# Seven products of ones on TensorE ahead of the first column sum of a two-layer linear-attention and SwiGLU kernel

## Chip, cores and metric

The kernel runs on one core of one Trainium2 chip. The metric is the device time of one execution in microseconds (us), the median over several runs; lower is better. A profile is one further execution, recorded by the hardware profiler; its span goes from the first to the last instruction.

## What is computed

The input x has 2048 rows of 512 numbers in fp32. Two layers are applied, each an attention block and an MLP block with the same weights:

```python
x = x + attention(layernorm(x), wqkv, wo)
x = x + mlp(layernorm(x), w1, w3, w2)
x = x + attention(layernorm(x), wqkv, wo)
x = x + mlp(layernorm(x), w1, w3, w2)

# attention, 32 heads of 16; phi(t) = where(t > 0, t + 1, exp(t)) + 1e-6
kv  = einsum("bhsd,bhse->bhde", phi(k), v)
z   = einsum("bhsd->bhd", phi(k))          # column sums over all rows
num = einsum("bhqd,bhde->bhqe", phi(q), kv)
den = einsum("bhqd,bhd->bhq", phi(q), z) + 1e-6
attention = (num / den) @ wo
# mlp, 512 -> 1792 -> 512
mlp = (silu(x @ w1) * (x @ w3)) @ w2
```

## The kernel before, in words

Every matmul operand is split into a high and a low half in fp16, and each product is made of three passes (high x high, low x high, high x low); the helper `mm` at L518 issues these passes, so most matmuls of the trace carry that line.

Rows are worked on in 16 tiles of 128. In the attention of layer 0 a loop over the tiles t = 0 to 15 (the key loop in `attention`) does the following on TensorE for each tile: the key product into a fresh bank `pk` (12 matmuls of 128x512), then, for the tile before it, the column sums `z` as two matmuls of a matrix of ones against the high and the low half of phi(k) (`gram_sum`, L901, into the bank `pz`, which stays the same for the whole loop), then 12 matmuls that add phi(k) x normalised row into four banks `gt` (`gram`). For t = 0 there is only the key product, so the first sum stands behind the key products of t = 0 and t = 1. The first column sum has `start=True`: it overwrites the bank, the later ones add to it.

Between the key product and the sum, ScalarE and VectorE compute phi: three ACTIVATEs (L868, L869, L870), a combination on VectorE (L879), the cast to the scaled high half on ScalarE (L946, the first sum needs it) and the low half on VectorE (L961, the second sum needs it). In the same loop, other tiles are prepared: bn_stats and bn_aggr on VectorE (L480, L481), four small steps on GpSimd for the scale of the layer norm (L488 to L492), the normalise on ScalarE (L495), the split into halves and a transposing DMA.

The order of the work in both attention stages is written by hand: everything inside `in_order()` keeps, on each engine, the order in which the program issues it, also across what it traces before. The MLP stages are not inside it; there a planner (the tile framework with its timeline model) orders the instructions by priority and by the time at which the model thinks their inputs are ready.

Ahead of the key loop the program issues products of a matrix of ones (`keep_busy`, L1657, into a bank `warm` that nobody reads): 22 at the start and 10 after the first weight scale's product `pm_k`. The bank pool for `pk`, `pz`, `warm` and `pm_k` (`bank`) has four banks; `gt` comes from another pool of four.

Of the kernel before, what the change touches and what calls it, by code (L numbers as in the profile page):

```python
# [17 lines left out]
P = 128  # L18
# [70 lines left out]
def kernel(  # L89
# [10 lines left out]
    nc = tc.nc  # L100
# [26 lines left out]
    def acc_bank(name):  # L127
        return psum.tile([P, 512], F32, tag="acc", name=name)

    def bank(name):  # L130
        return psum.tile([P, 512], F32, tag="w", name=name)
# [170 lines left out]
    ones16 = const.tile([P, P], F16, name="ones16")  # L302
# [114 lines left out]
    def engine_of(what, i):  # L417
        table = {what: table_of(what, state["layer"])}
        return {"V": nc.vector, "P": nc.gpsimd, "A": nc.scalar}[table[what][i]]
# [52 lines left out]
    def ln_stats(t0, n):  # L472

        ln_moments(t0, n)
        ln_scale(t0, n)
# [37 lines left out]
    def mm(dst, lhs, rhs, n, first=True, last=True, shared=False):  # L513


        for k in range(n):
            for i, (a, b) in enumerate(PASSES):
                nc.tensor.matmul(  # L518
                    dst,
                    lhs(a, k),  # L520
                    rhs(b, k),
                    start=first and k == 0 and i == 0,
                    stop=last and k == n - 1 and i == len(PASSES) - 1,
                    skip_group_check=shared,
                )
# [197 lines left out]
    def fill(prep):  # L723

        at = state["fills"]
        state["fills"] += 1
        if prep is None and "rows" not in state:
            return
        for tasks in prep or ():
            tasks.calls += 1  # L730
        table = FILLS[0 if prep is not None else 1]
        for which in table[at].strip("-") if at < len(table) else "":
            if which == "r":
                if "rows" in state:
                    next(state["rows"], None)
            elif prep is not None:
                if which == "1":
                    settle()
                prep[int(which) - 1].step()

    def next_tick(prep):
        if prep is not None:
            for tasks in prep:
                tasks.tick += 1
# [117 lines left out]
    def phi_act(ps, u, eps, in_bank=False):  # L862

        e, r = f32("kept"), ps if in_bank else f32()
        if eps:
            nc.scalar.activation(e, ps, AF.Relu, scale=info["nuk"])  # L868
            nc.scalar.activation(r, ps, AF.Identity, scale=u, bias=one_eps)  # L869
            nc.scalar.activation(e, e, AF.Exp, scale=-1.0)  # L870
        else:
            nc.scalar.activation(e, ps, AF.Exp, scale=u)
            nc.scalar.activation(r, ps, AF.Relu, scale=u)
        return e, r

    def phi_sum(e, r, eps, to=None):
        to = e if to is None else to
        if eps:
            nc.vector.scalar_tensor_tensor(to, e, EPS, r, OP.add, OP.max)  # L879
        else:  # L880
            nc.vector.scalar_tensor_tensor(to, e, 1.0, r, OP.min, OP.add)
        return to

    def attention(layer, ready, prep, before_gram):
# [5 lines left out]
        gt, pz, pks = [], [], {}  # L890
# [6 lines left out]
        def gram_sum(t):  # L897
            if sums[t] == "E":
                pk = pks[t]
                for a in range(2):  # L900
                    nc.tensor.matmul(  # L901
                        pz[0],
                        ones16,
                        pk[:, a, :],
                        start=t == sums.index("E") and a == 0,
                        stop=not rows_of and t == NT - 1 and a == 1,
                    )

        def gram(t):
            pk, nat = pks.pop(t), nats.pop(t)  # L910
            for j in range(NK):
                mm(
                    gt[j],
                    lambda a, k: nat[:, a, j * P : (j + 1) * P],
                    lambda b, k: pk[:, b, :],
                    1,
                    first=t == 0,
                    last=t == NT - 1,
                )

        for t in range(NT):
            if t:
                next_tick(prep)
            if layer == 0 and t == 12:
                nc.sync.dma_start(att_d["k"], wk_s)
            xt = xts.pop(t)
            pp = bank("pk")
            mm(pp, lambda a, k: xt[:, a * NK + k, :], lambda b, k: wk_s[:, b, k, :], NK)
            before_gram(t)
            if t == lag:  # L930
                gt.extend([acc_bank(f"gt{j}") for j in range(NK)])
                if "E" in sums:
                    pz.append(bank("pz"))
                for i in range(lag):
                    gram(i)
            if lag < t < LATER:
                gram_sum(t - 1)
                gram(t - 1)
            elif t > LATER:
                gram_sum(t - 2)  # L940
                gram(t - 2)
            e, r = phi_act(pp, info["uk"], True)
            pk = pks[t] = pk_ring.next(F16, 2, D)

            def high():
                nc.scalar.activation(pk[:, 0, :], e, AF.Copy, scale=info["tk"])  # L946
                if sums[t] != "E":
                    engine = engine_of("pz", t)
                    if t == rows_of[0]:
                        engine.tensor_copy(pksum, e)  # L950
                    else:
                        engine.tensor_tensor(pksum, pksum, e, OP.add)

            def turn():
                if t + 3 < NT:
                    keys_turn(t + 3, xts, nats)
                elif t + 3 - NT < 3:
                    load_query(t + 3 - NT)

            def low():  # L960
                nc.vector.scalar_tensor_tensor(  # L961
                    pk[:, 1, :], e, info["tk"], pk[:, 0, :], OP.mult, OP.subtract
                )

            steps_ = {
                "r": lambda: t + 3 < NT and keys_rows(t + 3),
                "s": lambda: phi_sum(e, r, True),
                "h": high,
                "t": turn,
                "l": low,  # L970
                "n": lambda: t + 4 < NT and ln_stats(t + 4, 1),
                "f": lambda: fill(prep),
            }
            for name in (KEYS[layer] if layer or t > 1 else FIRST[t]).split():
                steps_[name]()
# [147 lines left out]
    def keys_rows(t, xn=None):  # L1123

        xn = f32() if xn is None else xn
        xns[t] = xn
        normalise(xn, t)
# [3 lines left out]
    def keys_turn(t, xts, nats):  # L1131

        xn = xns.pop(t)
        xts[t] = xk_ring.next(F16, 2 * NK, P)
        nats[t] = nat = ring["nat"].next(F16, 2, D)
        high_part("key", t, nat[:, 0, :], xn)
        engine_of("keylow", t).tensor_tensor(nat[:, 1, :], xn, nat[:, 0, :], OP.subtract)
        last["t"] = nc.sync.dma_start_transpose(xts[t], nat.rearrange("p a d -> p (a d)"))
        keep_transposed(t, xts[t])
        issue_loads(t)  # L1140
# [27 lines left out]
    def load_query(t):  # L1168
        xqs[t] = xq_ring.next(F16, 2 * NK, P)
        nc.sync.dma_start(xqs[t], xt_d[:, t])  # L1170
# [288 lines left out]
    def pair(layer, ready, prep, before_gram):  # L1459
        state["layer"] = layer  # L1460
        if layer == 0 or PIN1:
            with in_order():
                attention(layer, ready, prep, before_gram)
        else:
            attention(layer, ready, prep, before_gram)
        return mlp(layer, prep)
# [175 lines left out]
    for item in LOADS[0].split():  # L1642
        what, t = item.split(":")
# [100 lines left out]
```

## Time and profile before

| | us |
|---|---|
| median of 3 runs | 1183.33 |
| lowest and highest run | 1180.77, 1184.78 |
| the profiled execution, its own time | 1182.41 |
| the profiled execution, span | 1180.7 |
| TensorE matmuls busy | 1148.0 (97%) |
| VectorE, ScalarE, GpSimd busy | 831.0, 638.8, 420.6 |
| mean granted TensorE clock | 0.999 |

In the rows below PE is TensorE's matmuls, PEld its weight loads, DVE VectorE, ACT ScalarE, POOL GpSimd, SP SyncE. A row of the view in order of time merges neighbouring instructions of one kind: start, duration of the whole merged piece, engine, line, operation, output<-inputs, shape, count, and in brackets the idle time of the engine before it and what ended that. A matmul's duration includes its way through the array, so consecutive ones overlap: their step from start to start is shorter than the duration of one.

### The profile page before, as it was taken

To read this page: it belongs to the slowest core of one execution; us is meant where nothing else is said; L and a number is where in the kernel's file an instruction comes from. 1 tells how busy PE (TensorE), PEld (TensorE's weight loads), DVE (VectorE), ACT (ScalarE), POOL (GpSimd) and SP (SyncE) were. 2 spreads that over 40 slices of the span, in tenths; PEclk is the share of its full clock that TensorE was granted. 3 is DMA by queue.
4 is the path that set the end of the run, shared out by engine and by line. 5 is a ranking of instruction groups with operands and counts; after the bars stand their busy time and mean duration, and the time that the engine had idled before them with its cause. 6 is when DMAs were issued, how large, how long until landed. Compare 5 with 4: busy or idle time off the path is not lost.

```text
span 1180.7 us, 21818 instructions
## 1 busy us (share of the span) xinstructions
PE 1148.0 (97%) x8868; PEld 863.3 (73%) x8868; DVE 831.0 (70%) x1383; ACT 638.8 (54%) x1078; POOL 420.6 (36%) x488
## 2 busy tenths in 40 slices
PE   8999998899999999999999999999999999999998
PEld 3444444788888888888864454467888888888887
DVE  6778898977877886767774559756855775756543
ACT  5777687856544454434456644775544344443422
POOL 5342589402000144235268714684542210102010
PEclk9999999999999999999999999999999999999999
DMA  8977575979542221111416434664351350121000
GB/s 258 342 207 245 113 171 110 270 246 294 159 143 99 81 81 64 63 64 64 81 53 180 103 110 105 130 156 112 99 139 64 126 188 26 57 79 37 1 37 37
DMA packets 163396, 147.43 MB, mean 125 GB/s; under 512 B 129632, under 2 KB 138976, under 8 KB 158688
## 3 DMA queue, kind: packets, MB, share of 16 engines
q1 hardware_dynamic: 163296, 146.04, 42.7%
q8 instruction: 69, 1.13, 0.4%
q14 instruction: 31, 0.25, 0.1%
HBM read 72.48 MB, written 42.07 MB: 97 GB/s over the span
## 4 chain that ended last, share of the span: by engine, by line
PE 60%; DVE 15%; ACT 7%; POOL 6%; DMA 6%; issue 3%; SPq 1%; POOLq 0%; ACTq 0%; DVEq 0%
PE bb L518 16%; PE po L1381 13%; PE bc L518 8%; PE gt L518 5%; PE pk L518 5%; PE ba L518 4%; PE po L518 3%; PE pq L518 3%; DMA arena<-arena 3%; DMA arena<-in_B_w_dram 3%; PE po L1401 2%; DVE arena L1290 2%; DVE arena L1337 2%; DVE arena L442 2%; DVE arena L1430 2%
## 5 line engine op out<-in xcount | busy, mean ns | idle before, releaser
L518 PEld LDWEIGHTS <-arena 128*128 128x128 f16 x6360 | 618.3, 98 | 257.0 <-issue 16.1
L518 PE MATMUL bb<-arena 128*128 128x256 f16 x2688 | 329.5, 273 | 6.6 <-ACT arena L1334 4.0
L1381 PE MATMUL po<-arena 128*128 128x256 f16 x1932 | 234.6, 273 | 9.0 <-ACT arena L1293 6.4
L1381 PEld LDWEIGHTS <-arena 128*128 128x128 f16 x1932 | 187.8, 98 | 35.5 <-ACT arena L1293 9.3
L1295 DVE TENSOR_TENSOR arena<-arena 128x512 f16<-128x512 f32 (+1 forms) x104 | 114.5, 1100 | 105.5 <-ACT arena L1293 105.2
L1334 ACT ACTIVATE arena<-bb 128x512 f32<-128x512 f32 x196 | 114.8, 589 | 122.8 <-PE bb L518 82.1
L518 PE MATMUL bc<-arena 128*128 128x256 f16 x1344 | 165.8, 273 | 0.7 <-ACT arena L1334 0.5
L1293 ACT ACTIVATE arena<-arena 128x512 f16<-128x512 f32 x112 | 99.8, 891 | 120.4 <-DVE arena L1308 46.9
L1289 ACT ACTIVATE arena<-arena,scalars 128x512 f32<-128x512 f32 x112 | 74.7, 667 | 116.0 <-DVE arena L1337 115.5
L1290 DVE SCALAR_TENSOR_TENSOR arena<-arena,scalars 128x512 f32<-128x512 f32 x112 | 88.5, 790 | 51.7 <-ACT arena L1289 51.6
L1337 DVE TENSOR_TENSOR arena<-arena,bc 128x512 f32<-128x512 f32 x112 | 76.5, 683 | 55.0 <-ACT arena L1334 44.4
L1450 POOL TENSOR_TENSOR arena<-arena 128x512 f32<-128x512 f32 x25 | 35.2, 1409 | 207.6 <-DVE arena L1430 207.6
L1430 DVE SCALAR_TENSOR_TENSOR arena<-po,scalars,arena 128x256 f32<-128x256 f32 (+1 forms) x170 | 92.1, 585 | 9.1 <-PE po L1381 7.6
L518 PE MATMUL pk<-arena 128*128 128x512 f16 x384 | 89.8, 384 | 2.2 <-DMA arena<-arena 2.1
L518 PE MATMUL po<-arena 128*128 128x512 f16 x384 | 87.8, 379 | 3.2 <-DMA arena<-arena 2.1
L518 PE MATMUL gt<-arena 128*128 128x512 f16 x384 | 87.8, 379 | 0.6 <-ACT arena L946 0.4
L518 PE MATMUL pq<-arena 128*128 128x512 f16 x384 | 87.6, 379 | 0.1
L518 PE MATMUL ba<-arena 128*128 128x256 f16 x672 | 87.1, 273 | 0.0
L1305 POOL TENSOR_TENSOR arena<-arena 128x256 f32<-128x256 f32 x15 | 11.9, 792 | 148.7 <-DVE arena L1290 148.7
L495 ACT ACTIVATE arena<-arena,nb_all,rs_all 128x512 f32<-128x512 f32 x64 | 50.5, 807 | 26.5 <-POOL nb_all L492 26.3
L1401 PE MATMUL po<-arena 128*128 128x256 f16 x480 | 56.8, 273 | 0.4 <-ACT arena L1293 0.4
L1276 POOL TENSOR_TENSOR arena<-arena 128x512 f16<-128x512 f32 (+2 forms) x33 | 47.4, 1460 | 26.0 <-DMA arena<-arena 19.8
(163 smaller groups left out, 1289.4 us busy)
## 6 DMA issues: line engine op xcount, KB each, us to landing
arena<-xb_d SPq DMA_DIRECT2D x12, 1792.0 KB, 7.1
xb_d<-arena SPq DMA_DIRECT2D x8, 1792.0 KB, 5.9
xt_d<-arena SPq DMA_DIRECT2D x32, 256.0 KB, 2.9
arena<-xt_d SPq DMA_DIRECT2D x32, 256.0 KB, 3.3
arena<-in_B_w_dram SPq DMA_DIRECT2D x8, 896.0 KB, 6.7
arena<-in_B_w_dram SPq DMA_DIRECT2D x28, 256.0 KB, 3.4
w_d<-arena SPq DMA_DIRECT2D x4, 1792.0 KB, 10.8
arena<-w_d SPq DMA_DIRECT2D x4, 1792.0 KB, 6.7
```

The costliest lines, as they stand in the source:

```text
L495: nc.scalar.activation(dst, x_sb[:, t, :], AF.Identity, scale=rs_all[:, t : t + 1], bias=nb_all[:, t : t + 1],)
L518: nc.tensor.matmul(dst, lhs(a, k), rhs(b, k), start=first and k == 0 and i == 0, stop=last and k == n - 1 and i == len(PASSES) - 1, skip_g ...
L1276: engine_of("rowlow", 2 * c + j).tensor_tensor(nat[:, 1, lo:hi, :], s, nat[:, 0, lo:hi, :], OP.subtract)
L1289: nc.scalar.activation(t, gate, AF.Silu, scale=info["u1"])
L1290: nc.vector.scalar_tensor_tensor(t, up, info["hid"], t, OP.mult, OP.mult)
L1293: nc.scalar.activation(hs[:, 0, lo:hi], t[:, lo:hi], AF.Copy)
L1295: engine.tensor_tensor(hs[:, 1, lo:hi], t[:, lo:hi], hs[:, 0, lo:hi], OP.subtract)
L1334: nc.scalar.activation(dst, bank_, AF.Copy)
L1337: nc.vector.tensor_tensor(dst, dst, bank_, OP.add)
L1381: nc.tensor.matmul(po[:, i * HALF : (i + 1) * HALF], hs[:, a, qx, cs], w2[:, b, qw, :], start=g == ends[0] and i + a + b == 0, stop=g == e ...
L1401: nc.tensor.matmul(acc[n][:, half * HALF : (half + 1) * HALF], hs[:, a, qx, cs], w2_a21[g][:, b] if (i, half) == (0, 1) else w2[:, b, i + ...
L1430: nc.vector.scalar_tensor_tensor(dst, src, cb, to, OP.mult, OP.add)
```

## The change

At t = 1 of layer 0's key loop, behind the key products and ahead of the first column sum, seven products of ones with ones are issued into the bank `pz`. Each starts and stops its own accumulation, and the first column sum, which has `start=True`, overwrites what they leave.

```diff
                 for i in range(lag):
                     gram(i)
+            if layer == 0 and t == 1:
+
+                for _ in range(7):
+                    nc.tensor.matmul(
+                        pz[0].rearrange("p (a n) -> p a n", a=4),
+                        ones16,
+                        ones16[:, None, :].to_broadcast([P, 4, P]),
+                        start=True,
+                        stop=True,
+                    )
             if lag < t < LATER:
                 gram_sum(t - 1)
                 gram(t - 1)
```

## Rows read from the trace of the kernel before

**Rows 1.** The page: busy time by engine, and the clock in 40 slices.
```profile
PE 1148.0 (97%) x8868; PEld 863.3 (73%) x8868; DVE 831.0 (70%) x1383; ACT 638.8 (54%) x1078; POOL 420.6 (36%) x488
...
PEclk9999999999999999999999999999999999999999
```

**Rows 2.** TensorE's matmuls in order of time, 12 to 26 us.
```profile
12.17 5.35 PE L518 MATMUL pk<-arena 128*128 128x512 f16 x24
19.40 0.38 PE L901 MATMUL pz<-arena,ones 128*128 128x512 f16 x1 [1.88 <-ACT arena L946]
20.19 0.38 PE L901 MATMUL pz<-arena,ones 128*128 128x512 f16 x1 [0.41 <-DVE arena L961]
20.40 2.75 PE L518 MATMUL gt<-arena 128*128 128x512 f16 x12
22.99 2.75 PE L518 MATMUL pk<-arena 128*128 128x512 f16 x12
```

**Rows 3.** The chain that ended last, 15 to 26 us: start, us, what.
```profile
15.44 0.60 DVE st L480
...
17.70 0.20 POOL nb_all L492
...
17.93 0.81 ACT arena L495
18.74 0.62 ACT arena L946
...
19.39 0.76 DVE arena L961
...
20.19 0.38 PE pz L901
20.57 2.59 PE gt L518 x12
23.16 2.59 PE pk L518 x12
```

**Rows 4.** All engines in order of time: the products of ones at the start.
```profile
3.78 0.15 PEld L1657 LDWEIGHTS <-ones 128*128 128x128 f16 x1 [0.28 <-issue]
4.21 0.15 PEld L1657 LDWEIGHTS <-ones 128*128 128x128 f16 x1 [0.28 <-issue]
...
9.71 2.32 PE L1657 MATMUL warm<-ones 128*128 128x512 f16 x10
```

**Rows 5.** The line of the sums: operation, count, ns min/median/max, first and last start.
```profile
L901 PE MATMUL pz<-arena,ones x32: 376/379/379, 19.4 to 106.9; 128*128 128x512 f16 x32
```

**Rows 6.** Stretches around the wait: busy us of PE, PEld, DVE, ACT, POOL; PEclk; DMA share; GB/s.
```profile
12.00:17.50 5.50, 5.36 (x25) 2.37 (x25) 4.67 (x15) 4.62 (x8) 2.17 (x4) 1.00 0.83 228
17.50:20.20 2.70, 0.41 (x3) 0.10 (x2) 1.60 (x4) 2.27 (x4) 1.62 (x4) 1.00 1.07 286
20.20:26.00 5.80, 5.80 (x27) 2.63 (x27) 2.14 (x4) 2.56 (x5) 3.15 (x6) 1.00 1.01 328
```

**Rows 7.** ScalarE in order of time, 14 to 24 us.
```profile
15.55 0.77 ACT L869 ACTIVATE arena<-pk,scalars 128x512 f32<-128x512 f32 x1
...
18.65 0.70 ACT L946 ACTIVATE arena<-arena,scalars 128x512 f16<-128x512 f32 x1
19.26 0.67 ACT L868 ACTIVATE arena<-pk,scalars 128x512 f32<-128x512 f32 x1
```

**Rows 8.** TensorE in order of time at 44 us.
```profile
44.72 4.45 PE L518 MATMUL pk<-arena 128*128 128x512 f16 x12 [2.08 <-DMA arena<-arena]
```

**Rows 9.** Stretches of half a us there, columns as in rows 6.
```profile
44.50:45.00 0.50, 0.28 (x2) 0.17 (x3) 0.42 (x1) 0.50 (x2) 0.00 (x0) 1.00 1.03 393
45.00:45.50 0.50, 0.50 (x4) 0.24 (x3) 0.50 (x2) 0.44 (x2) 0.00 (x0) 0.85 1.06 406
45.50:46.00 0.50, 0.50 (x3) 0.20 (x2) 0.47 (x2) 0.50 (x2) 0.00 (x0) 0.50 1.03 397
...
48.50:49.00 0.50, 0.50 (x3) 0.14 (x2) 0.50 (x2) 0.00 (x0) 0.00 (x0) 0.73 1.33 352
49.00:49.50 0.50, 0.50 (x4) 0.25 (x3) 0.50 (x1) 0.29 (x1) 0.00 (x0) 1.00 1.02 386
```

**Rows 10.** TensorE in order of time at 199 us.
```profile
199.58 1.25 PE L518 MATMUL bb<-arena 128*128 128x256 f16 x10 [2.07 <-DMA arena<-arena]
200.67 1.26 PE L518 MATMUL ba<-arena 128*128 128x256 f16 x10
```

**Rows 11.** The stretch behind it, columns as in rows 6.
```profile
199.50:204.00 4.50, 4.42 (x41) 3.96 (x41) 3.27 (x8) 3.32 (x7) 4.50 (x5) 1.00 0.52 117
```

**Rows 12.** TensorE's waits from 200 us to the end: us in total, times, longest.
```profile
PE po L1381 <- ACT arena L1293: 6.4, 9, 1.8
PE bb L518 <- ACT arena L1334: 4.0, 5, 1.6
```

## Prediction

> **What bounds the kernel now.** I read the page first: its table of busy time, the clock row of its 40 slices, then the waits of TensorE, and only then the microseconds around the edit. The page says that TensorE's matmuls are busy for 97% of the span and that no other engine passes 70% [rows 1]. So a change in the number or the place of matmuls counts where TensorE is late, and is free where it sits idle. The edit stands in the key loop of layer 0 at t = 1, between the 24 products of the first two key tiles and the first column sum. TensorE's rows in order of time show the place: the `pk` products run from 12.17 us and end at 17.52, then the engine is idle for 1.88 us until the first sum starts at 19.40, idle again for 0.41 us, and the second sum starts at 20.19 with the twelve `gt` products right behind it [rows 2]. The chain that ended last tells what the two waits are: it does not run through TensorE before 20.19. It runs through bn_stats of tile 3, GpSimd's four small steps, ScalarE's normalise at L495, its key cast at L946 (0.62 us on the chain) and VectorE's low part at L961 (0.76 us), and only then through the second sum [rows 3]. L495 and L946 sit in ScalarE's queue in that order, so the first sum waits for a normalise of another tile, not for more matmul time. TensorE's idleness here is a symptom; filling it shortens none of these steps.
>
> **The change, part by part.** It removes nothing and moves nothing. It adds seven matmuls of 128x512 with their seven weight loads, on TensorE alone: no DMA, nothing on VectorE, ScalarE, GpSimd or SP.
>
> Their price: the same form stands in the kernel as `warm`. Ten of them, at the clock's upper level, took 2.32 us in all [rows 4], and one alone lasts 379 ns by the row of the sums [rows 5], so the step from start to start is (2.32 - 0.38) / 9 = 0.216 us. Seven cost 7 x 0.216 = 1.51 us of issue. The first can start one step after the last `pk` product started, 17.52 - 0.38 + 0.216 = 17.36 us; the seventh starts at 17.36 + 6 x 0.216 = 18.65 and ends at 19.03. The first sum is released at 19.40, 0.37 us after that. **Cost on the path: 0.** What hides them is the 1.88 us wait, and if that cover shrank there is a second one: the second sum is held by L961 until 20.19, so the first sum could start as late as 20.19 - 0.216 = 19.97 for nothing. Seen from the step at which the queue is free (18.87), the cover left is 19.97 - 18.87 = 1.10 us, five more products.
>
> The bound above: the products at the lower level of 1.2 GHz. At the start of the kernel weight loads of the same stream are 0.42 to 0.43 us apart [rows 4]. Seven at 0.43: the seventh starts at 17.36 + 6 x 0.43 = 19.94, the first sum at 20.37, the second at 20.80, against 20.19: 0.61 us late. I take the upper level, since the granted clock is 1.00 in the stretch before, in it and after it [rows 6], and the 24 products before it ran at it, (5.35 - 0.38) / 23 = 0.216 us apart [rows 2]; 0.61 us stays for the range.
>
> Waits added: the seven write a bank that was handed out at t = 0 and that nobody reads before the end of the loop; their operand `ones16` was set at the start. The two tiles made in `bank` before the key tiles, `warm` and `pm_k`, end by 9.71 + 2.32 = 12.03 us [rows 4], and the first two `pk` tiles are alive beside it. The sum that follows is on the same engine and starts its bank anew. So the wait for L946 stays where it is, on the first sum, and the seven stand before it in the queue. Bound of an unseen wait: the bank could at worst be free when ScalarE's reads of the first key tile end (15.55 + 0.77 = 16.32) [rows 7], still before 17.36. Cost 0. Nor does anyone wait for the seven: ScalarE takes the second key tile only at 19.26, behind L946 [rows 7], although its products ended at 17.52.
>
> What they could give is the clock, and here the trace has three waits of about this size. After 2.08 us of idleness TensorE resumed at 44.72; the granted clock fell to 0.50 soon after and came back at about 48.8, and the twelve products took 4.45 us [rows 8, 9] instead of the 2.75 us of the same row elsewhere [rows 2]: 1.70 us lost. After 2.07 us, ended at 199.58, the clock stayed at 1.00 and the products ran at full speed [rows 10, 11]. After our 1.88 + 0.41 us it stayed at 1.00 too [rows 6], and the `gt` and `pk` rows behind it read 2.75 us [rows 2]. So equal idleness can end either way, and in this execution there is nothing at this place to win back. **Gain: 0 here; up to 1.70 us in an execution where the clock does fall here.** I take 0, the row of this very place, and keep 1.70 for the range.
>
> The Trainium skill, in "TensorE: Matmul & The Clock Gate", Part 1, under "What's actually happening", says that the window in which the chip judges activity runs free and does not restart with a kernel. That agrees with the two waits of 2.07 and 2.08 us that ended differently. By that rule the same wait may lose the clock in one execution and keep it in the next, and the sum would be 0 in some and -1.70 us in others; the profile shows one execution only.
>
> **Sum.** 1182.41 us (the profiled execution, span 1180.7 plus 1.7 around it) + 0 - 0 = 1182.4 us. That is 0.9 below the median of the three runs, 1183.33, and inside their spread of 1180.77 to 1184.78.
>
> **The rivals.**
>
> *A: the fall of the clock at this place is usual, and the change removes it.* For: the three runs spread over 4.0 us, more than two falls at 1.70; one of the three similar waits shows a fall, and ours is in two pieces, so the whole of it (17.52 to 20.19) is the longest thin stretch of the three: TensorE is busy for 0.41 of 2.70 us in it [rows 6]. Against: the only execution I can see keeps the clock. If the median run of before holds the fall, after is 1183.33 - 1.70 = 1181.6 us. Behind 20.19 the chain is TensorE's through the sums, `gt` and `pk` [rows 3], so the loss would be carried on.
>
> *B: slower, by the order of the MLP.* Only the attention stages are written in a fixed order; the MLP's instructions are ordered by a planner with a timeline model of its own. If the model believes that the seven products push TensorE back, the instructions of the MLP could come out in another order. The price is bounded by the largest waits of TensorE there, 6.4 us for L1293's cast ahead of the output products and 4.0 us for L1334's copies [rows 12]; an order that doubles both gives 1182.4 + 10.4 = 1192.8 us. It decides as soon as TensorE's idle time before L1381 and `bb` grows by 3.5 us. Against: the seven lie on one engine, in a wait, with a fixed order over the whole attention stage that follows, so all engines should enter the MLP as before.
>
> *C: the same with the other sign.* An order that halves both waits gives 1182.4 - 5.2 = 1177.2 us. It needs the same accident.
>
> *D: the change doesn't do what it says:* the seven run at the lower level, or wait for the bank, and hold the sums back. By the bound above this is +0.6 us, 1183.0, inside what can be told from nothing.
>
> **How the numbers follow.** Forecast (nothing moves), 1182.4 us: 0.58. A, 1181.6: 0.22. D, 1183.0: 0.05. B, 1192.8: 0.08. C, 1177.2: 0.07. A measurement of this kernel tells some 0.3%, 3.5 us, from no change. Only C and B lie beyond that, so faster 0.07, slower 0.08, same 0.85. The range: the lowest run shown less one fall avoided, 1180.77 - 1.70 = 1179.1, to the highest run shown with one more fall elsewhere, 1184.78 + 1.70 = 1186.5. It holds the forecast, A and D, 0.85 in all, and leaves B and C out.
>
> **What would show it.** In the trace of after: a row of seven matmuls into `pz` from `ones` between 17.3 and 19.1 us, the first sum at 19.40 and the second at 20.19 as before, the `gt` and `pk` rows behind them at 2.75 us, TensorE's busy time up by about 1.5 us and its wait for L946 down from 1.88 to about 0.4 us, with the span unmoved. The weight loads of the seven should be some 0.2 us apart. The fall of the clock after 44.72 may or may not be there. Wrong it would be if the sums start later than 20.19 (cost of the products), if the same fall is gone from later stretches with the time down by 1.70 us or a multiple (A, more widely than I think), or if the output products' waits in the MLP differ by more than a few tenths (B, C).

## The result and the profile after

Twenty runs of each kernel: before 1181.91 us in the median, after 1184.39 (1182.19 to 1187.36). The ratio is 1.0018, with a 95% interval of 1.0012 to 1.0025: the change costs some 2 us. That is less than the 3.5 us that the prediction called "no change", but it is clear of the noise of so many runs. The profiled execution of after took 1186.52 us (span 1184.7).

The lines that answer to [rows 2] and [rows 8], TensorE's matmuls of after in order of time (start us, us, what, count, and in brackets the idle time before and what ended it):

```profile
17.22 1.67 PE L939 MATMUL pz<-ones 128*128 128x512 f16 x7
19.26 0.38 PE L901 MATMUL pz<-arena,ones 128*128 128x512 f16 x1 [0.37 <-ACT arena L956]
20.05 0.38 PE L901 MATMUL pz<-arena,ones 128*128 128x512 f16 x1 [0.41 <-DVE arena L971]
20.26 2.75 PE L518 MATMUL gt<-arena 128*128 128x512 f16 x12
...
29.12 2.76 PE L518 MATMUL pk<-arena 128*128 128x512 f16 x12 [0.49 <-DMA arena<-arena]
...
47.41 4.45 PE L518 MATMUL pk<-arena 128*128 128x512 f16 x12 [3.76 <-DMA arena<-arena]
```

The first four rows are as forecast: the seven take 1.67 us, end 0.37 us ahead of the first sum, and the second sum still starts 0.79 us after the first. (The line numbers of after are 10 higher behind the edit.) What differs comes 9 and 27 us later. The `pk` products of t = 3, which waited for nothing in before, wait 0.49 us for their transposing DMA, and those of t = 6 wait 3.76 us instead of 2.08 and start at 47.41 us instead of 44.72: 2.69 us late. The program order of every engine is the same in both kernels but for the seven products and their weight loads, the waits as well. So this is no new order (rivals B and C are out); a transfer has become later.

Which one, the first reader of the first w1 block on VectorE tells. The block is 896 KB of the MLP's weights, which the key loop loads ahead; the reader is L360, a maximum over the block, and it stands in VectorE's queue ahead of the key tile's phi. First before, then after:

```profile
27.20 2.08 DVE L360 TENSOR_REDUCE pt_w<-arena 128x1 f32<-128x896 f32 x2 [0.47 <-DMA arena<-in_B_w_dram]
```
```profile
28.21 2.08 DVE L360 TENSOR_REDUCE pt_w<-arena 128x1 f32<-128x896 f32 x2 [1.64 <-DMA arena<-in_B_w_dram]
```

The block lands 1.0 us later, and VectorE, whose queue is in order, hands that on to L879, to the statistics and the keys of the next tiles, and through these to the issue of later DMAs. And SyncE (SPq is its queue), which issues all DMAs, is held longer by a transposing DMA of that time. First before, then after:

```profile
25.97 1.34 SPq L1138 DMA_TRANSPOSE arena<-arena  x1
28.24 0.33 SPq L1156 DMA_DIRECT2D xt_d<-arena  x1
```
```profile
25.82 2.42 SPq L1148 DMA_TRANSPOSE arena<-arena  x1
29.13 0.33 SPq L1166 DMA_DIRECT2D xt_d<-arena  x1
```

How that becomes 2.69 us at t = 6 stands in SyncE's rows and in the chain that ended last. SyncE issues a further block of weights (L533) and then the transposing DMA of t = 6 (L1138, L1148 in after). First before, then after; the last line of each is that DMA's way from issue to landing:

```profile
37.32 0.46 SPq L533 DMA_DIRECT2D arena<-in_B_w_dram  x1
38.86 1.23 SPq L1138 DMA_TRANSPOSE arena<-arena  x1
...
38.86 5.81 DMA arena<-arena
```
```profile
38.72 0.45 SPq L533 DMA_DIRECT2D arena<-in_B_w_dram  x1
39.28 2.15 SPq L1148 DMA_TRANSPOSE arena<-arena  x1
...
39.28 8.09 DMA arena<-arena
```

The transposing DMA is issued only 0.42 us later, but lands at 47.37 instead of 44.67 us, 2.70 us later. In all fourteen profiled executions of this document it lands 0.8 to 1.0 us behind the block issued ahead of it. That block is issued 1.40 us later, and it takes 7.68 instead of 6.54 us (by its landing in the trace's semaphore records). Why it takes 1.14 us longer, no run shows; the next fetch of TensorE's program lies at 58.5 us in both.

One thing in the DMA queues had moved. The page's DMA part counts a queue `q8 instruction`, with 69 packets of 16 KB; TensorE has 17736 matmuls and weight loads, 257 to a packet, so I take these packets for TensorE's own program. In the stretch from 24.5 to 27 us (queue and kind: packets, MB, share of 16 engines), before shows no such packet, and after shows one; from 28 to 30.5 us it is the other way round. First after at 24.5 to 27, then before at 28 to 30.5:

```profile
q1 hardware_dynamic: 562, 0.73, 150.6%
q8 instruction: 1, 0.02, 2.3%
```
```profile
q1 hardware_dynamic: 378, 0.99, 100.2%
q8 instruction: 1, 0.02, 2.4%
```

2.3% of 16 engines for 2.5 us is 0.92 us of one DMA engine. The seven products are 14 instructions (a weight load and a matmul each), and with 14 more ahead of it TensorE's stream asks for a 16 KB block earlier: at 24.92 us, amid the first w1 block and the transposing DMA of t = 3, instead of at 28.52, behind both (they landed at 27.17 and 28.18). The other instruction queue, q14, is no such sign: its packet near 40 us starts at 41.6 us in before and at 39.7 in e5_count, which are equally fast.

The clock: after shows a fall behind the wait near 47 us, like before, and none near 20 us. In this execution a second one follows at 235 us, behind a wait of 2.59 us for L1344. The kernel is 2.69 us behind where the first `kv` product starts (120.96 against 118.26 us), and 4.08 us behind at the last matmul (1180.67 against 1176.60); the 1.4 us between come with that second fall. Such a fall near 235 us also stands in e2_after and e7_fillB_after below, but not in e11_after nor in any of the other ten executions; so it may well have a part in the median, which the profiles can't tell.

### The profile page after: what moved, and what is told of

Same layout as the page of the kernel before. It is cut to its first block, busy times and chain, and to the rows that moved or that the text cites. A ratio compares the mean times of both kernels' runs of the same rounds, so it can differ in the third digit from the quotient of the medians.

```text
span 1184.7 us, 21832 instructions
## 1 busy us (share of the span) xinstructions
PE 1152.1 (97%) x8875; PEld 865.3 (73%) x8875; DVE 830.6 (70%) x1383; ACT 637.7 (54%) x1078; POOL 420.5 (35%) x488
## 4 chain that ended last, share of the span: by engine, by line
PE 62%; DVE 15%; DMA 7%; ACT 7%; POOL 4%; issue 3%; SPq 2%; POOLq 0%; ACTq 0%; DVEq 0%
PE bb L518 16%; PE po L1391 13%; PE bc L518 8%; PE pk L518 5%; PE gt L518 5%; PE po L518 5%; PE pq L518 4%; PE ba L518 4%; DMA arena<-arena 3%; DMA arena<-in_B_w_dram 3%; PE po L1411 2%; DVE arena L1300 2%; DVE arena L1347 1%; DVE arena L442 1%; DVE arena L1440 1%
## 5 line engine op out<-in xcount | busy, mean ns | idle before, releaser
L1344 ACT ACTIVATE arena<-bb 128x512 f32<-128x512 f32 x196 | 114.7, 588 | 122.9 <-PE bb L518 82.8
L1347 DVE TENSOR_TENSOR arena<-arena,bc 128x512 f32<-128x512 f32 x112 | 76.4, 682 | 55.5 <-ACT arena L1344 44.9
```

The lines of the kernel that those rows point to most:

```text
L1344: nc.scalar.activation(dst, bank_, AF.Copy)
L1347: nc.vector.tensor_tensor(dst, dst, bank_, OP.add)
```

## The experiments

Two theories were put to the test. **T, the traded fall:** the thin stretch near 20 us does make the clock fall in many executions of before, but the time lost comes out of the later wait, and the change only moves the fall there. **F, the moved fetch:** the 14 further instructions move a program fetch into the critical transfers. The rivals stand with each expectation. Every kernel does the whole computation; only products that nobody reads are added or taken away. F came up after the first four runs; theory I of these four (the instructions themselves do harm) is its forerunner.

**e1_before, e2_after.** The two kernels once more.

> The kernel before once more, with its clock in every run. Theory T (traded fall): the thin stretch between 17.5 and 20.2 us costs before a fall of the clock in a good part of its executions, that fall is absorbed by the later 2 us wait for the transposing DMA, and executions with it show no second fall at 45 us; so its runs show one fall (mean clock 0.999) or none, seldom two, median about 1181.9 us. Theory I (more instructions): the mean clock is no different from that of after.

> The changed kernel once more. Theory T: median about 1184.4 us, the clock lower than in before by one fall in many runs (0.997 to 0.998), a fall behind the wait near 45 us, none near 20 us. Theory I (the 14 further instructions themselves do harm): 1184.4 us too, whatever the clock does.

Measured: e1_before 0.9995 of before [0.9985, 1.0005], e2_after 1.0014 [1.0006, 1.0023]. Over these twelve runs of each kernel the mean clocks are the same, 0.998. Over all runs on record they are not: 0.9987 for before (108 runs) and 0.9981 for after (40 runs). One fall costs 1.70 us, 0.0014 of the span, so after has some 0.4 of a fall more in a run (an estimate from these numbers). What also differs is where the falls lie. This execution of the unchanged kernel has the fall near 20 us:

```profile
19.27 0.38 PE L901 MATMUL pz<-arena,ones 128*128 128x512 f16 x1 [1.88 <-ACT arena L946]
20.06 0.38 PE L901 MATMUL pz<-arena,ones 128*128 128x512 f16 x1 [0.41 <-DVE arena L961]
20.28 4.44 PE L518 MATMUL gt<-arena 128*128 128x512 f16 x12
...
44.53 2.76 PE L518 MATMUL pk<-arena 128*128 128x512 f16 x12 [0.39 <-DMA arena<-arena]
```

The `gt` products lose 1.69 us (4.44 against 2.75), and the wait near 45 us shrinks by the same 1.69 (0.39 against 2.08), so that TensorE resumes at 44.53, no later than the 44.72 of [rows 8], and no fall follows there. The span is 1178.8 us, 1.9 less than that of before's first profile, which had the fall behind the wait. In this execution the fall near 20 us is not only free, it goes with none near 45. (A later one, at 197.9 us, costs 1.71 us in its rows, and the two waits for L1334 and L1235 behind it shrink from 1.01 + 1.16 us in before to 0.59 in all.)

**e3_tiny7, e4_four.** The edit with seven products of 16 columns, and with four full products.

```diff
-                for _ in range(7):
+                for _ in range(4):          # e4_four
...
-                        pz[0].rearrange("p (a n) -> p a n", a=4),
+                        pz[0][:, :16],      # e3_tiny7
                         ones16,
-                        ones16[:, None, :].to_broadcast([P, 4, P]),
+                        ones16[:, :16],     # e3_tiny7
```

> The seven products with 16 columns instead of 512: the same instructions in number, order, bank and waits, but next to no time of the array, so the idle stretch stays. Theory T: like before, about 1182 us (within 0.7). Theory I (instructions, bank or queue do the harm): like after, about 1184.4 us.

> Four products instead of seven: the idle stretch before the first sum is 1.0 us instead of 0.4 us. Theory T: the fall behind it becomes rare already, so like after or in between, 1183 to 1184.4 us. Theory I: in between by number, 1183.3 us.

Measured: e3_tiny7 1.0003 [0.9991, 1.0016], e4_four 1.0012 [1.0001, 1.0023]. By its time e3_tiny7 is as T had it, 1182.84 us beside 1182.60 of before, although its interval reaches up to the lower half of after's; e4_four fits both. So the times speak for T, if anything. But the traces give what was missing: in e3_tiny7 the clock fell at 19.8 us, as in e1_before, and yet the wait near 45 us was 1.93 us and not 0.4. The fetch is at 25.67 us here and at 26.06 in e4_four. Something that comes with the instructions and not with their array time seemed to make transfers late.

**e5_count.** The seven products stay; 14 instructions go from the start, where 22 products of ones become 9 and three fp32 products (an fp32 product is two weight loads and two matmuls, and about four times as long: five take 4.45 us in e6_long_count).

```diff
-        keep_busy(22)
+        keep_busy(9)
+        for _ in range(3):
+            nc.tensor.matmul(
+                warm.rearrange("p (a n) -> p a n", a=4),
+                ones,
+                ones[:, None, :].to_broadcast([P, 4, P]),
+                start=True,
+                stop=True,
+            )
```

> The changed kernel, but of the 22 products of ones at the start 13 are replaced by three fp32 products of about the same total time, which takes 14 instructions out of TensorE's stream ahead of the seven: its 16 KB instruction fetches should be back where before has them. Theory F (moved fetch): in before that fetch lies near 28.5 us, in after near 24.9, amid the load of the first w1 block and a transposing DMA; with the count restored it lies at 28.5 again, the w1 block lands near 27.2, the wait ahead of the pk products at 45 us is about 2 us instead of 3.4 to 3.8, and the time is 1.5 us below after, about 1182.5 us. Rival (the fetch is a bystander, only the clock matters): 1184 us as after, wait of 3 us or more.

Measured: 1.0000 of before [0.9991, 1.0009], 1181.73 us beside 1181.34. The fetch is back behind 28 us (the q8 line is of the stretch 28 to 30.5), the block lands when it did, and the wait is 2.47 us:

```profile
q8 instruction: 1, 0.02, 2.7%
```
```profile
27.00 2.08 DVE L360 TENSOR_REDUCE pt_w<-arena 128x1 f32<-128x896 f32 x2 [0.61 <-DMA arena<-in_B_w_dram]
```
```profile
17.28 1.67 PE L939 MATMUL pz<-ones 128*128 128x512 f16 x7
19.07 0.38 PE L901 MATMUL pz<-arena,ones 128*128 128x512 f16 x1
...
44.93 4.45 PE L518 MATMUL pk<-arena 128*128 128x512 f16 x12 [2.47 <-DMA arena<-arena]
```

With the count of instructions restored, the seven products cost nothing and bring nothing: the forecast of the prediction, but for the fetch. F's rival, as it was put (1184 us and a wait of 3 us or more), falls. The clock did change, too: its mean is 0.9994 over these twelve runs, against 0.9987 of before on the same chip. So the products do take falls away, and the time shows nothing of it.

**e9_tinystart.** The reverse: before, with 14 instructions of next to no array time at the start, far from the first sum.

```diff
         keep_busy(22)
+        for _ in range(7):
+            nc.tensor.matmul(warm[:, :16], ones16, ones16[:, :16], start=True, stop=True)
```

> The kernel before, with seven products of 16 columns behind the 22 products of ones at the start, and nothing at the first sum: 14 instructions more ahead, next to no time of the array, the idle stretch left open. Theory F (moved fetch): the 16 KB fetch moves from 28.5 to about 25 us, the w1 block lands about 1 us later (28 us), the wait near 45 us is longer by 1 us or more, and the runs are slower than before by 0.1 to 0.2%, 1 to 2 us. Rival (the seven full products themselves are to blame): as before, ratio 1.000.

Measured: 1.0011 [1.0001, 1.0022], 1183.02 us beside 1181.72: slower, without any product at the first sum, though the interval only just leaves 1 out. The fetch is at 24.82 us, the block lands at 29.3, and although the clock fell near 20 us in this execution, the wait near 48 us is 3.35 us and a second fall follows:

```profile
29.34 2.08 DVE L360 TENSOR_REDUCE pt_w<-arena 128x1 f32<-128x896 f32 x2 [2.80 <-DMA arena<-in_B_w_dram]
```
```profile
20.23 4.44 PE L518 MATMUL gt<-arena 128*128 128x512 f16 x12
...
48.12 4.31 PE L518 MATMUL pk<-arena 128*128 128x512 f16 x12 [3.35 <-DMA arena<-arena]
```

**e6_long_count.** Five fp32 products hold the first sum back; the start, whose edit is like that of e5_count and is left out here, gives back their 20 instructions (2 fp16 and 5 fp32 products there).

```diff
-                for _ in range(7):
+                for _ in range(5):
                     nc.tensor.matmul(
                         pz[0].rearrange("p (a n) -> p a n", a=4),
-                        ones16,
-                        ones16[:, None, :].to_broadcast([P, 4, P]),
+                        ones,
+                        ones[:, None, :].to_broadcast([P, 4, P]),
```

> Five fp32 products in place of the seven, some 4.3 us long, which hold the first sum back by about 1.7 us as a fall of the clock there would, but at full clock; the start is again in fp32 so that the instruction count ahead equals that of before. Theory T (traded fall: time lost here is given back at the wait near 45 us, and what costs is the clock that falls behind that wait): wait near 45 us about 0.4 us, no fall there, the time that of the faster executions of before, about 1180.5 us, in most runs. Rival (TensorE's time here counts): 1.7 us above e5_count, about 1184.

Measured: 0.9995 [0.9986, 1.0004], 1181.14 us, 0.6 below e5_count of the same chip.

```profile
17.23 4.45 PE L939 MATMUL pz<-ones 128*128 128x512 f32 x10
21.52 0.59 PE L901 MATMUL pz<-arena,ones 128*128 128x512 f16 x2
...
44.59 2.76 PE L518 MATMUL pk<-arena 128*128 128x512 f16 x12 [0.46 <-DMA arena<-arena]
```

The sums run together at 21.52 us, the second 1.9 us after its place in e5_count (19.86), and the wait near 45 us takes it back: 0.46 against 2.47 us. TensorE resumes at 44.59, and no fall follows there. The time lies 3 us below the rival's 1184; that it is below e5_count's is within the noise. So TensorE's time near 20 us is worth nothing up to some 2 us; T's first half holds.

**e7_fillB_after, e8_fillB_before, e12_best.** Two fp32 products ahead of the `pk` products of t = 6, in their own bank, put into after, into before, and into e5_count.

```diff
             pp = bank("pk")
+            if layer == 0 and t == 6:
+                for _ in range(2):
+                    nc.tensor.matmul(
+                        pp.rearrange("p (a n) -> p a n", a=4),
+                        ones,
+                        ones[:, None, :].to_broadcast([P, 4, P]),
+                        start=True,
+                        stop=True,
+                    )
             mm(pp, lambda a, k: xt[:, a * NK + k, :], lambda b, k: wk_s[:, b, k, :], NK)
```

> The changed kernel, with two fp32 products of ones (some 1.7 us) also ahead of the pk products of t = 6, in their own bank, which fill half of the wait near 45 us. Theory T: the fall behind that wait becomes rare, at most 1.7 us saved on after in the runs that have it: about 1182.7 us, still above before by the longer wait. Rival (the fall there costs nothing): 1184 us as after.

> The kernel before with these two fp32 products ahead of the pk products of t = 6, and nothing else. Theory T: executions whose clock falls near 20 us lose up to 1.3 us (their wait is only 0.4 us), the others win 1.7 us; median 1181 us, with less scatter than before. Rival: no change, 1182.

> Seven products ahead of the first sum, the start's 22 with 14 instructions fewer (as e5_count), and two fp32 products ahead of the pk products of t = 6: no fall of the clock near 20 us nor near 45 us, the fetch where before has it. Both theories: 1180.5 to 1181 us, 1 us below before, with less scatter. Rival (the falls cost nothing): 1182 as e5_count.

Measured: e7_fillB_after 1.0007 [0.9996, 1.0017], e8_fillB_before 0.9991 [0.9983, 1.0000], e12_best 0.9989 [0.9981, 0.9998] (1180.38 us beside 1181.72, its runs within 1179.18 to 1181.51 where before's spread over 1180.08 to 1184.5). In e12_best the products stand in the wait, and the clock keeps its level:

```profile
42.29 1.88 PE L930 MATMUL pk<-ones 128*128 128x512 f32 x4
44.89 2.76 PE L518 MATMUL pk<-arena 128*128 128x512 f16 x12 [0.72 <-DMA arena<-arena]
```

The fall near 45 us is worth about what it costs in the rows, 1.7 us: of the six executions with the fetch behind 28 us, the four without it start the first `kv` product at 116.4 to 116.7 us, the two with it (before, e5_count) at 118.3 and 118.5. e12_best is 1.3 us below before in the median (1181.72 to 1180.38), just clear of the noise, and so below both kernels. The 8 further instructions of these edits also move the second fetch, in e8_fillB_before and e12_best from 58.5 to 55.5 us; but e1_before and e6_long_count, without that fall, are as far ahead with it at 58.3. e7_fillB_after gains some 1 us on after by the ratios (1.0007 against 1.0014 to 1.0018), which its interval doesn't tell from none.

**e10_more, e11_after.** After with 46 more instructions at the start (23 products of 16 columns), and after alone on the same chip.

```diff
         keep_busy(22)
+        for _ in range(23):
+            nc.tensor.matmul(warm[:, :16], ones16, ones16[:, :16], start=True, stop=True)
```

> The changed kernel with 23 products of 16 columns behind the start, 46 instructions more, 60 in all against before. Theory F: what counts is where the fetch falls, not how many instructions there are; it should move to about 20 us, ahead of the critical load and transposing DMA, the w1 block lands near 27 us again, wait near 45 us about 2 us, and the time is 1 to 2 us below after, near 1182.5. Rival (every further instruction costs): slower than after.

> The changed kernel once more, for comparison on this chip: 0.15% above before, fetch near 25 us, w1 block near 28 us, wait near 45 us above 3 us.

Measured: e11_after 1.0017 [1.0004, 1.0029]; e10_more 1.0049 [1.0036, 1.0062], 1187.37 us. My expectation was wrong. The fetch did not go to 20 us but to 16.26, and there it meets the transposing DMA of tile 2 (SyncE's row of it, where before has 1.24 us at 16.04):

```profile
15.72 2.30 SPq L510 DMA_TRANSPOSE arena<-arena  x1
```

Everything that SyncE issues behind it is late: the first w1 block is issued at 21.12 instead of 20.40 us and lands at 28.5, and the wait near 47 us is 3.74 us. The fetch again stands beside a transposing DMA that holds SyncE longer. But by its time this run fits the rival, "every further instruction costs", and it doesn't part the two. Its 5.6 us are more than these rows explain: in the profile 2.8 us have gathered by the first `kv` product (121.05 against 118.26), the rest comes later, a fall at 835.9 us among it.

All profiled executions side by side (start of the first 16 KB fetch in the trace's DMA records; first reader of the w1 block; wait ahead of `pk` of t = 6 and that row's start):

| kernel | TensorE's instructions ahead of the fetch, against before | fetch, us | reader starts, us | wait, us | resumes, us | ratio to before |
|---|---|---|---|---|---|---|
| before | 0 | 28.52 | 27.20 | 2.08 | 44.72 | |
| e1_before | 0 | 28.62 | 26.93 | 0.39 | 44.53 | 0.9995 |
| e8_fillB_before | 0 | 28.24 | 27.09 | 0.42, half filled | 44.74 | 0.9991 |
| e5_count | 0 | 29.03 | 27.00 | 2.47 | 44.93 | 1.0000 |
| e6_long_count | 0 | 29.60 | 27.07 | 0.46 | 44.59 | 0.9995 |
| e12_best | 0 | 29.28 | 27.01 | 0.72, half filled | 44.89 | 0.9989 |
| e4_four | 8 | 26.06 | 28.12 | 2.45 | 46.00 | 1.0012 |
| e3_tiny7 | 14 | 25.67 | 27.56 | 1.93 | 45.94 | 1.0003 |
| e9_tinystart | 14 | 24.82 | 29.34 | 3.35 | 48.12 | 1.0011 |
| after | 14 | 24.92 | 28.21 | 3.76 | 47.41 | 1.0018 |
| e2_after | 14 | 24.76 | 27.80 | 3.38 | 46.61 | 1.0014 |
| e11_after | 14 | 25.20 | 29.03 | 3.63 | 48.10 | 1.0017 |
| e7_fillB_after | 14 | 26.07 | 28.29 | 1.94, half filled | 47.39 | 1.0007 |
| e10_more | 60 | 16.26 | 28.47 | 3.74 | 47.65 | 1.0049 |

Six executions with the fetch behind 28 us resume at 44.5 to 44.9 us, whatever the clock did; eight with an earlier one resume at 45.9 to 48.1. The ratios follow less closely: that of e3_tiny7, 1.0003, can't be told from 1.

## Why the prediction was wrong

The time lies in the range (1184.39 in 1179.1 to 1186.5) and the change is below the 3.5 us, but the kernel did get slower, and the forecast was that nothing moves.

- **The price of the seven products was right.** 1.67 us of work between 17.22 and 18.9, the first sum 0.37 us later, nothing on the path; e5_count shows it as a time, 1.0000 of before.
- **The step that failed** is the first of "The change, part by part": "on TensorE alone: no DMA". TensorE's program is itself brought by DMA. The trace of before has that queue, `q8 instruction` with 69 packets on the page, and I took it for nothing. The term of 0 for DMAs should have been bounded by these rows: 14 instructions ahead can move a later fetch, a fetch is 0.9 us of a DMA engine, and between 20 and 45 us the key tiles wait for transfers. Measured, it is some 2 us in the ratio, and in the profiles the landing that ends the wait at t = 6 is 2.70 us later (47.37 against 44.67). What TensorE loses ahead of that wait, 0.49 us at t = 3 and 0.39 at the sum behind it, adds nothing, since it resumes when that DMA lands. How much of the 2 us is the later landing itself and how much is falls behind longer waits, the runs don't part: the mean clock is 0.9981 in after and 0.9994 in e5_count, some 0.9 of a fall a run (an estimate as above).
- **The Trainium skill** has a rule that spoke to this and that I had not weighed. "Runtime: NRT & Kernel Launch", section "Instruction fetch mechanics", says that each engine's program is refilled in 16 KiB blocks of 256 instructions over a DMA queue of its own, and that crossing a block boundary is mostly hidden. The packets of 16 KB and 257 instructions agree. "Hidden" holds for TensorE, which shows no stall at the fetch of 24.92 us (its `pk` products start at 22.85 us and the next sum follows at 25.44, as in before); for the transfers beside it, it doesn't: after and e5_count have the same products and the fetch on either side of them, and stand at 1.0018 and 1.0000 of before.
- **Rival A was half right.** The fall near 20 us is common: it stands in three of five profiled executions with the stretch left open (e1_before, e3_tiny7 and e9_tinystart; not in before and e8_fillB_before), and in none of the nine with four or more full products there. But its price was wrong. I argued that the loss "would be carried on", since the chain behind 20.19 us is TensorE's [rows 3]; that chain ends 25 us later in a wait for a DMA [rows 8], which takes the loss back. The 1.70 us was not there to win. e5_count shows it as a time: fewer falls than before, and no gain.
- **Two waits of equal length that ended differently** [rows 8 to 11] were read rightly: two executions of one program, before and e1_before, have their falls at different places. The Trainium skill's free-running window (TensorE: Matmul & The Clock Gate, Part 1) agrees.
- **No rival had a cost of this size:** D stood at +0.6 us and B at +10.4, so 2 us from DMAs had no place between them.
- **B and C** did not happen; the order is the same on all engines. D did not either.

Left open: by what way the fetch makes the others late. The times of e5_count and e9_tinystart show that it is the number of instructions that costs, not the products' time on TensorE (that of e3_tiny7 leaves it open), and the traces that the fetch and the late transfers go together in all fourteen executions. That the fetch is what makes them late is an inference. The record shows a packet of 0.9 us on one DMA engine at the time at which the w1 block and a transposing DMA drag on. A share that queues behind it on that engine alone would come late alone; but the block's 16 parts land within 0.10 us of each other in before (27.07 to 27.17) and in after (28.09 to 28.19). Nor was a kernel tried that has more instructions and its fetch in a harmless place (e10_more was meant as one and was not), which would part the place of the fetch from the count.

## What to carry to other kernels

Products that filled idle time of TensorE were free on TensorE, but each is two instructions, and further instructions can move a later program fetch; where transfers are tight, look up where the fetches fall before and after, and try giving the instructions back elsewhere. Before filling a wait to keep the clock up, follow the loss to the next wait behind it: if that wait takes it back, there is nothing to win; filling that later wait is what paid here, if little (e8_fillB_before 0.9991 [0.9983, 1.0000], e12_best 0.9989 [0.9981, 0.9998]).

## What the runs showed of the hardware

- A packet of the queue `q8 instruction` is 16 KB; the one followed here takes 0.92 to 1.29 us. In the eight executions with it ahead of 27 us the transposing DMA issued near 26 us holds SyncE for 1.65 to 3.19 us, in the six others for 1.23 to 1.61, and the first reader of an 896 KB load starts at 27.56 to 29.34 us instead of 26.93 to 27.20.
- 14 instructions moved that fetch by 3.6 us (28.52 to 24.92) although they are 1.5 us of work. In the six executions with the count of before it starts 0.2 to 1.6 us behind the landing of the key tile of t = 3 (27.9 to 28.2 us), also in e1_before, whose `pk` products ahead of it run 1.56 us later than in before; that it is held until then is an inference.
- A fall of the granted clock from 1.00 to 0.50 costs the rows behind it 1.7 us. The one near 20 us cost the kernel nothing in e1_before, where a wait for a DMA follows (0.39 instead of 2.08 us), and went with none behind that wait; in e9_tinystart, where that wait was 3.35 us, a fall followed even so.
